# Attention in a two-layer block on one core: a semaphore between half products, two exponentials in one, and block results copied by two engines

## The chip, the cores and the metric

The kernel runs on one core of a Trainium2 chip. The metric is the device time of one execution in microseconds. The kernel before takes 3538.99 us (median of 3 runs, 3538.1 to 3539.18).

## The reference

Four stages follow each other, with the same weights in both rounds: attention, a perceptron with squared relu, attention, the perceptron again.

```python
def _A_ref(x, wqkv, wo):                 # S=2048 rows, D=640, H=32 heads of 20
    qkv = (x @ wqkv).reshape(B, S, 3, H, Dh).transpose(2, 0, 3, 1, 4)
    q, k, v = qkv[0], qkv[1], qkv[2]
    scores = jnp.einsum("bhqd,bhkd->bhqk", q, k) * (Dh ** -0.5)
    p = _softmax(scores, axis=-1)
    o = jnp.einsum("bhqk,bhkd->bhqd", p, v)
    return o.transpose(0, 2, 1, 3).reshape(B, S, D) @ wo
...
x = A_x
x = x + _A_ref(_layernorm(x, axis=-1), A_wqkv, A_wo)
x = x + _B_ref(_layernorm(x, axis=-1), B_w1, B_b1, B_w2, B_b2)   # relu(x w1 + b1)^2 w2 + b2
x = x + _A_ref(_layernorm(x, axis=-1), A_wqkv, A_wo)
x = x + _B_ref(_layernorm(x, axis=-1), B_w1, B_b1, B_w2, B_b2)
```

## The kernel before

All is float32. Products that need the accuracy are made from a high and a low part of each operand.

Only the attention is touched by the change. It runs over 32 blocks in each layer. A block `t` is a group of four heads and 512 queries, and it goes through 16 key tiles of 128 keys. The passage of one key tile is called a step here. A step holds:

- four score products, one for each head of the group (`score`, the product is line 596). The 128 keys of the tile are the stationary operand, the 512 queries the moving one. A head has 62 rows in the contraction: 60 of the high and low parts, and 2 that subtract the row's maximum. Heads 0 and 2 lie on partitions 0 to 63 of the array, heads 1 and 3 on partitions 64 to 127, so two products run beside each other. The results go to PSUM banks 0 to 3, in turn (`ps_st`).
- four exponentials on ScalarE (line 603), one for each of these banks, 128 x 512 each, into the tiles `e`.
- the weighted values of the step before (`pv`, line 608): for each head the 128 x 32 values against the exponentials. The four heads take four groups of 32 columns of the array, and all add up in bank 7 over the 16 steps of a block. One row of each group adds up the exponentials, which the division needs.
- products for the row maxima of later blocks (`by_queries`, line 481), with queries as stationary operand and keys as moving one, in banks 4 to 6. VectorE takes the maximum of each. In a step there are two products over 512 keys, one on either half of the partitions (`smax`, the maximum is line 493), and two half products over 256 keys each, which share one bank (`smax_half`, line 521): the first half product fills the left half of the bank from partitions 0 to 63, the second the right half from partitions 64 to 127.

The order of all these instructions is written out by hand, since TensorE takes its instructions in the order of the program. The table `ORDERS` holds strings. In a string `a` is the next score on partitions 0 to 63 (head 0, then head 2), `b` the next on partitions 64 to 127 (head 1, then head 3), `m` and `n` are the full products for maxima on partitions 0 to 63 and 64 to 127, `u` and `w` the two half products on partitions 0 to 63 and 64 to 127, and `V` is `pv` for the step before. The string in use nearly everywhere is number 12, and eight of its letters and a `V` make up a step:

```python
12: "mbubanawV" * 8,
```

Between `u` and `w` stands an instruction without work on VectorE: the function `smax_half` puts a `nop` there that waits for `u` (line 517 in the profile), and `w` waits for this `nop`. Two products from different halves of the partitions may not write to one bank at the same time, and this keeps them apart.

At the end of a block `finish` copies bank 7 to the tile `o` (line 621, on ScalarE; on VectorE for the last block of a layer), and later steps send out the row of sums, invert it and multiply. The next block's first `V` writes to bank 7 again, so it waits for the copy. `op` in `attention` calls all of this, one letter at a time; `both_heads` (line 1158 and, for its exponential over two banks, line 1165) serves the last block of a layer alone.

Of the kernel before, what the change touches and what calls it, by code (L numbers as in the profile page):

```python
# [10 lines left out]
AF = mybir.ActivationFunctionType  # L11
# [13 lines left out]
QB = 512  # L25
# [7 lines left out]
SCALE = DH ** -0.5  # L33
NBLK = NG * NQB
# [5 lines left out]
def tile_layers(  # L40
# [11 lines left out]
    nc = tc.nc  # L52
# [10 lines left out]
    def name(p):  # L63
        n_alloc[0] += 1
        return f"{p}{n_alloc[0]}"

    def slot(shape, dtype, label):
        return arena.tile(shape, dtype, tag="slot", name=name(label))

    def dma(eng, dst, src):  # L70

        if dst.dtype == F32R:
            dst = dst.bitcast(F32)
        if src.dtype == F32R:
            src = src.bitcast(F32)
        eng.dma_start(dst, src)
# [4 lines left out]
    banks = psum.tile([P, 8, 512], F32, tag="banks", name="banks")  # L81
# [11 lines left out]
        def coming(self, k):  # L93
            return [self.order[(self.n + 1 + i) % len(self.order)] for i in range(k)]

    ps_st = Ring(0, 1, 2, 3)
    ps_pj = Ring(4, 5, 6, 7)
    ps_q = Ring(0, 1, 2, 3)
    ps_all = Ring(0, 1, 2, 3, 4, 5, 6, 7)
# [154 lines left out]
    def split_to(dst_hi, dst_lo, src):  # L254

        nc.scalar.copy(dst_hi, src)
        nc.vector.tensor_sub(dst_lo, src, dst_hi.bitcast(F32))  # L257
# [12 lines left out]
    def pool_hi(dst, src):  # L270
        nc.gpsimd.tensor_copy(dst, src)  # L271
# [31 lines left out]
    def after(later, earlier, reason="one half of the rows adds to the bank that the other half has left"):  # L303
        tc.add_manual_dep(
            later.ins,
            earlier.ins.name,
            mybir.DependencyInfo(mybir.DependencyClass.Sync, mybir.DependencyReason.DATA),
            reason=reason,
        )
# [115 lines left out]
    weights, e_n = [], []  # L425
# [45 lines left out]
    def maxima(t):  # L471
        if t not in mx_t:
            mx_t[t] = small.tile([P, 4, 4, 6], F32, tag="mx", bufs=14, name=name("mx"))
            if t in PARTLY:
                nc.vector.memset(mx_t[t][:, :, :, :4], LEAST)
        return mx_t[t]

    def by_queries(dst, t, p, sub, c, par, keys=slice(0, QB)):

        b = 64 * par  # L480
        return nc.tensor.matmul(  # L481
            dst,
            q_t[t][b : b + 60, p, sub * P : (sub + 1) * P],
            k_t[t // NQB, c][b : b + 60, p, keys],
            start=True,
            stop=True,
        )
# [7 lines left out]
        )  # L495

    halved = {}

    def two_columns(t):

        if t not in halved:
            halved[t] = True
            nc.gpsimd.memset(maxima(t)[:, :, :, 4:], LEAST)

    def column(*x):

        halved[x] = halved.get(x, 3) + 1
        assert halved[x] < 6
        return halved[x]

    def smax_half(bank, t, p, sub, c, half, par, earlier=None):

        w = QB // 2
        dst = bank[:, par * w : (par + 1) * w]
        m = by_queries(dst, t, p, sub, c, par, slice(half * w, (half + 1) * w))
        if earlier is None:
            mark = nc.vector.nop()
            after(mark, m)
            return mark
        after(m, earlier, "matmuls on two halves of the rows write to one bank in turn")  # L520
        nc.vector.tensor_reduce(  # L521
            maxima(t)[:, p : p + 3 : 2, sub, c if not half else column(t, p, sub)],
            bank.rearrange("q (r k) -> q r k", r=2),
            axis=AX.X,
            op=ALU.max,
        )

    def step_one(t, p, sub, x, par):

        dst = ps_q("sm")  # L530
        res = xtile("rl")[:, :QB]
        by_queries(dst, t, p, sub, x, par)
        nc.scalar.activation(res, dst, AF.Relu)  # L533
        return res
# [48 lines left out]
        done.add(t)  # L583

    free = []

    def score(t, kt, h, es):

        p, par = divmod(h, 2)
        if p not in es:  # L590
            es[p] = weights[len(e_n) % len(weights)]
            e_n.append(t)
        dst = banks[:, free.pop(0), :] if free else ps_st("st")
        b = 64 * par
        assert t in done
        nc.tensor.matmul(  # L596
            dst,
            k_t[t // NQB, kt // 4][b : b + 62, p, (kt % 4) * P : (kt % 4 + 1) * P],
            q_t[t][b : b + 62, p, :],
            start=True,  # L600
            stop=True,
        )
        nc.scalar.activation(es[p][:, par, :], dst, AF.Exp, scale=SCALE)  # L603

    def pv(acc, t, kt, es, heads=(3, 2, 1, 0)):
        for h in heads:
            p, par = divmod(h, 2)
            nc.tensor.matmul(  # L608
                acc[32 * h : 32 * h + 32, :],
                v_t[t // NQB, kt // 8][:, kt % 8, 32 * h : 32 * h + 32],  # L610
                es[p][:, par, :],
                start=(kt == 0),
                stop=(kt == NKT - 1),
            )

    def finish(t, acc):


        g, qb = divmod(t, NQB)
        o = slot([P, 2, QB], F32, "o")  # L620
        (nc.vector.tensor_copy if t == NBLK - 1 else nc.scalar.copy)(o[:, 0, :], acc)
        res = []

        def store(q):
            ot = res.pop().rearrange("p l t -> p (l t)")
            for h in range(4):
                r0 = (4 * g + h) * DH
                dma(q, d_o[r0 : r0 + DH, qb], ot[32 * h : 32 * h + DH])

        if t == NBLK - 1:  # L630

            def invert():
                dst = ps_all("rs")
                nc.tensor.matmul(dst, sums_t, o[:, 0, :], start=True, stop=True)
                nc.vector.reciprocal(o[:, 1, :], dst)

            def divide():
                nc.vector.tensor_mul(o[:, 0, :], o[:, 0, :], o[:, 1, :])
                res.append(slot([P, 2, QB], F32R, "ot"))
                split_to(res[0][:, 0, :], res[0][:, 1, :], o[:, 0, :])  # L640

            return [invert, divide, lambda: store(nc.scalar)]

        few = small.tile([P, 16], F32, tag="few", bufs=2, name=name("few"))
        for h in range(4):
            dma(nc.sync, d_s[t, h : h + 1], o[32 * h + DH : 32 * h + DH + 1, 0, :])

        def load():
            dma(nc.sync, few, d_s[t].rearrange("h (q j) -> (h q) j", j=16))

        def invert():
            nc.gpsimd.tensor_tensor(few, few, minus_t, op=ALU.pow)  # L652

        def spread():
            dma(nc.sync, d_r[t].rearrange("h (q j) -> (h q) j", j=16), few)

        def gather():
            for h in range(4):
                dma(nc.sync, o[32 * h : 32 * h + 32, 1, :], d_r[t, h].partition_broadcast(32))

        def divide():
            ot = slot([P, 2, QB], F32R, "ot")
            nc.gpsimd.tensor_mul(o[:, 0, :], o[:, 0, :], o[:, 1, :])
            pool_hi(ot[:, 0, :], o[:, 0, :])
            pool_lo(ot[:, 1, :], o[:, 0, :], ot[:, 0, :].bitcast(F32))
            res.append(ot)

        return [load, invert, spread, gather, divide, lambda: store(nc.sync)]
# [46 lines left out]
    def qkv(first, x_src, rest, scores):  # L715
# [275 lines left out]
        15: "anbmnanbaabmbnammbnaVbmbmmbVmbananVanmbanVnambmbVanbmnaVnmbaanVmbbanmV",  # L991
        14: "mbbbanmbbmambmVanannaVmbnaaanVbmabnmVanbmbmbVnaanmbVmabmbanVbmannaVn",
        13: "baanmbVmbanambbnbmVanbmnaVnaabnmbVanbmaanVnmbbanaVmnbmabVabbmmnaVm",
        12: "mbubanawV" * 8,
    }

    def attention(first, x_src, first_rows):
# [8 lines left out]
        turn = [4, 5, 6]  # L1006
# [23 lines left out]
        rows = {"next": min(t for t in range(NBLK) if t not in done), "at": None}  # L1030
# [113 lines left out]
        def both_heads(p):  # L1144

            i = state["wide"]
            t, kt = divmod(i, NKT)
            if p == 0 and i > state["begun"]:
                state["begun"] = i
                begin(i)  # L1150
            es = es_of.setdefault(i, {})
            es[p] = weights[len(e_n) % len(weights)]
            e_n.append(t)
            state["bank"] = (state["bank"] + 2) % 6
            dst = banks[:, state["bank"] : state["bank"] + 2, :]
            for par in range(2):
                b = 64 * par
                nc.tensor.matmul(  # L1158
                    dst[:, par, :],
                    k_t[t // NQB, kt // 4][b : b + 62, p, (kt % 4) * P : (kt % 4 + 1) * P],  # L1160
                    q_t[t][b : b + 62, p, :],
                    start=True,
                    stop=True,
                )
            nc.scalar.activation(es[p], dst, AF.Exp, scale=SCALE)  # L1165
            if p:
                state["wide"] += 1

# [9 lines left out]
            state["debt"] -= n  # L1178
            return n

        free.extend((5, 6))
        for o in "abab":
            op(o)
        yield
# [12 lines left out]
        for p in (0, 1, 0):  # L1197
            both_heads(p)
# [361 lines left out]
```

## Time and profile before

| what | value |
|---|---|
| time of the kernel before, median of 3 | 3538.99 us |
| the profiled execution's own time | 3538.19 us |
| its span, first to last instruction | 3536.2 us |
| granted TensorE clock over the span | 1.000 |
| TensorE busy | 3521.2 us (100%) |
| TensorE weight loads busy | 2264.2 us (64%) |
| VectorE busy | 2731.2 us (77%) |
| ScalarE busy | 2652.9 us (75%) |

The two attention stages lie at about 310 to 1370 us and 2070 to 3130 us of the span. In rows of the profile, PE is TensorE's products and PEld its weight loads, DVE is VectorE, ACT is ScalarE, SP is SyncE, and DVEq is VectorE's sequencer, which runs waits. A row of a timeline gives the start in us from the beginning of the span, the length in us, the engine, the line, the operation, and what is written from what. `x2` behind a row means two instructions of the same kind that overlap or touch, shown as one bar. A bar of a product is partly modelled: its start is when TensorE took it up, which can be before its weights have arrived. Several waits have their arrow behind the bar: `[0.21 <-ACT o L621]` says that the engine stood idle for 0.21 us and that ScalarE's write of tile `o` in line 621 ended it.

### The profile page before, as it was taken

Reading aid. Unit: us, or ns where it says so; the run is one execution under the profiler, and the core shown is the slowest. Engines: PE = TensorE matmul, PEld = TensorE weight load, DVE = VectorE, ACT = ScalarE, POOL = GpSimd, SP = SyncE. Lnnn points to the kernel's source line nnn. Section 1 sums busy time; section 2 is a strip of 40 time slices with the busy share of each in tenths; the row PEclk is TensorE's granted clock in tenths of the full one; section 3 lists DMA queues with packets and bytes.
Section 4 is the critical chain, followed back from the end, with each engine's and each line's share of the span. In section 5 each row is a group of like instructions: output and inputs, shape, how many; then the busy total and the mean of one; then the engine's idle time right before and its main releaser. Section 6 shows DMA issues by size and latency. Waiting matters only on the chain.

```text
span 3536.2 us, 70757 instructions
## 1 busy us (share of the span) xinstructions
PE 3521.2 (100%) x26542; PEld 2264.2 (64%) x26542; DVE 2731.2 (77%) x5023; ACT 2652.9 (75%) x5208; POOL 809.5 (23%) x927
## 2 busy tenths in 40 slices
PE   9999999999999999999999999999999999999999
PEld 7897444444444446999988964444444444479998
DVE  8878999999999993456567789999999999824443
ACT  3778999999999995122237789999999999932221
POOL 6531444221221111111153201221211211211110
PEclk9999999999999999999999999999999999999999
DMA  9776555323211136734477652232232111376231
GB/s 304 274 233 175 172 156 157 109 70 82 57 48 49 46 110 209 249 106 111 135 269 249 197 150 76 65 82 61 67 82 59 46 48 43 115 226 238 75 82 38
DMA packets 377413, 452.78 MB, mean 128 GB/s; under 512 B 176642, under 2 KB 223746, under 8 KB 377070
## 3 DMA queue, kind: packets, MB, share of 16 engines
q1 hardware_dynamic: 376254, 445.89, 41.6%
q8 instruction: 209, 3.42, 0.4%
q10 hardware_dynamic: 816, 2.36, 0.2%
q14 instruction: 134, 1.10, 0.1%
HBM read 273.83 MB, written 174.30 MB: 127 GB/s over the span
## 4 chain that ended last, share of the span: by engine, by line
PE 95%; DVE 2%; ACT 1%; DMA 1%; issue 1%; POOL 0%; SPq 0%; DVEq 0%; ACTq 0%
PE banks L608 29%; PE banks L481 22%; PE banks L293 13%; PE banks L596 11%; PE banks L1326 10%; PE banks L331 9%; DVE mx L493 1%; ACT e L603 1%; PE banks L1158 0%; DMA q<-d_qk 0%; ACT e L1165 0%; DVE bst L244 0%; DVE xnT L257 0%; DVE x L252 0%; DMA d_qk<-ev 0%
## 5 line engine op out<-in xcount | busy, mean ns | idle before, releaser
L603 ACT ACTIVATE e<-banks 128x512 f32<-128x512 f32 x3968 | 2034.7, 613 | 10.3 <-PE banks L596 2.2
L493 DVE TENSOR_REDUCE mx<-banks 128x1 f32<-128x512 f32 x2094 | 1346.5, 686 | 187.2 <-PE banks L596 126.6
L481 PE MATMUL banks<-k,q 60*128 60x512 f32 x4568 | 1347.7, 374 | 3.0 <-DVE v L377 1.7
L481 PEld LDWEIGHTS banks<-k,q 60*128 60x128 f32 x4568 | 763.8, 184 | 848.5 <-DVE mx L493 824.8
L596 PE MATMUL banks<-q,k 62*128 62x512 f32 x3968 | 1132.1, 432 | 0.4 <-DVE mx L541 0.4
L608 PE MATMUL banks<-e,vg 128*32 128x512 f32 x8192 | 1091.0, 605 | 1.5 <-ACT e L1165 1.5
L596 PEld LDWEIGHTS banks<-q,k 62*128 62x128 f32 x3968 | 654.5, 184 | 99.8 <-ACT e L603 36.6
L521 DVE TENSOR_REDUCE mx<-banks 128x2 f32<-128x512 f32 x982 | 670.5, 683 | 0.0
L541 DVE CUSTOM_DVE_ANT_0 rl<-banks,rl 128x512 f32<-128x512 f32 x510 | 332.8, 689 | 101.1 <-PE banks L481 91.0
L1311 ACT ACTIVATE r<-banks,b_t 128x512 f32<-128x512 f32 x96 | 66.2, 689 | 420.1 <-PE banks L293 396.3
L331 PE MATMUL banks<-xnT,wqk 64*128 64x512 f32 x2400 | 378.8, 394 | 0.3 <-ACT mark_t L333 0.3
L533 ACT ACTIVATE rl<-banks 128x512 f32<-128x512 f32 x510 | 270.8, 597 | 98.2 <-PE banks L481 89.3
L1326 PE MATMUL banks<-w,h 128*128 128x320 f32 x2304 | 340.4, 309 | 0.0
L1326 PEld LDWEIGHTS banks<-w,h 128*128 128x128 f32 x2304 | 339.2, 188 | 1.2
L293 PE MATMUL banks<-xnT,w 128*128 128x512 f32 x1440 | 329.4, 389 | 0.0
L331 PEld LDWEIGHTS banks<-xnT,wqk 64*128 64x128 f32 x2400 | 286.1, 185 | 34.2 <-issue 2.4
L293 PEld LDWEIGHTS banks<-xnT,w 128*128 128x128 f32 x1440 | 269.6, 188 | 55.3
L608 PEld LDWEIGHTS banks<-e,vg 128*32 128x32 f32 x8192 | 161.1, 108 | 165.5 <-issue 78.4
L652 POOL TENSOR_TENSOR few<-few,minus_t 128x16 f32<-128x16 f32 x62 | 179.8, 2900 | 357.9 <-DMA few<-d_s 352.5
L271 POOL CAST mr<-nt 128x32 fp32r<-128x32 f32 x64 | 13.4, 209 | 963.7 <-DVE nt L567 963.7
L331 PE MATMUL banks<-wv,xnT 64*128 64x320 f32 x1920 | 199.4, 307 | 0.9 <-ACT mark_t L333 0.9
L331 PEld LDWEIGHTS banks<-wv,xnT 64*128 64x128 f32 x1920 | 187.3, 185 | 2.5 <-ACT mark_t L333 1.4
(89 smaller groups left out, 2094.2 us busy)
## 6 DMA issues: line engine op xcount, KB each, us to landing
q<-d_qk SPq DMA_DIRECT2D x242, 240.0 KB
d_qk<-ev SPq DMA_DIRECT2D x80, 512.0 KB
k<-d_qk SPq DMA_DIRECT2D x152, 240.0 KB
x<-d_x SPq DMA_DIRECT2D x84, 320.0 KB
d_qk<-ev SPq DMA_DIRECT2D x80, 256.0 KB
d_o<-ot SPq DMA_DIRECT2D x248, 80.0 KB
ot<-d_o SPq DMA_DIRECT2D x38, 512.0 KB
d_v<-v SPq DMA_DIRECT2D x32, 512.0 KB
```

The source lines that it names most:

```text
L293: nc.tensor.matmul(dst, a, b, start=(n == 0), stop=(n == last))
L331: m = nc.tensor.matmul(ch["dst"][:, :width], *pair, start=first, stop=last)
L481: return nc.tensor.matmul(dst, q_t[t][b : b + 60, p, sub * P : (sub + 1) * P], k_t[t // NQB, c][b : b + 60, p, keys], start=True, stop=True,)
L493: nc.vector.tensor_reduce(maxima(t)[:, 2 * par + p, sub, c : c + 1], dst, axis=AX.X, op=ALU.max)
L521: nc.vector.tensor_reduce(maxima(t)[:, p : p + 3 : 2, sub, c if not half else column(t, p, sub)], bank.rearrange("q (r k) -> q r k", r=2), ...
L533: nc.scalar.activation(res, dst, AF.Relu)
L541: nc.vector.tensor_tensor_reduce(out=r, in0=dst, in1=r, scale=1.0, scalar=LEAST, op0=ALU.add, op1=ALU.max, accum_out=maxima(t)[:, 2 * par ...
L596: nc.tensor.matmul(dst, k_t[t // NQB, kt // 4][b : b + 62, p, (kt % 4) * P : (kt % 4 + 1) * P], q_t[t][b : b + 62, p, :], start=True, stop ...
L603: nc.scalar.activation(es[p][:, par, :], dst, AF.Exp, scale=SCALE)
L608: nc.tensor.matmul(acc[32 * h : 32 * h + 32, :], v_t[t // NQB, kt // 8][:, kt % 8, 32 * h : 32 * h + 32], es[p][:, par, :], start=(kt == 0 ...
L652: nc.gpsimd.tensor_tensor(few, few, minus_t, op=ALU.pow)
L1326: nc.tensor.matmul(dst[:, :HALF], hs[f][:, hx, i * P : (i + 1) * P], w_2.piece(at_2(f0 + f, hw, hf)), start=(f == 0 and (hx, hw) == THREE[0]),
```

## The change

Four edits come together. First, the `nop` on VectorE between the half products goes. The first half product raises a semaphore of its own when it ends, and the second waits for that semaphore on TensorE. Second, the scores get fixed banks: head 1 bank 0, head 3 bank 1, head 0 bank 2, head 2 bank 3. Banks 1 and 2 lie side by side, and the exponentials of heads 3 and 0, which are the second and the third in the new order, become one instruction over 128 x 1024. Third, the order of a step becomes `bumbawnaV`. Fourth, at the end of a block VectorE copies the right half of bank 7's columns and ScalarE the left half. In the last block of a layer VectorE still copies all of it. At the start of an attention stage the first four scores use banks 5, 6, 0 and 1 explicitly, as the fixed banks need it.

```diff
-    ps_st = Ring(0, 1, 2, 3)
...
+    first_half = tc.alloc_semaphore("first_half")
+    firsts_done = [0]
...
         m = by_queries(dst, t, p, sub, c, par, slice(half * w, (half + 1) * w))
         if earlier is None:
-            mark = nc.vector.nop()
-            after(mark, m)
-            return mark
-        after(m, earlier, "matmuls on two halves of the rows write to one bank in turn")
-        nc.vector.tensor_reduce(
+            firsts_done[0] += 1
+            m.then_inc(first_half, 1)
+            tc.no_tile_sem_insts.add(m.ins.name)
+            tc.add_to_no_dep_group(f"first half {firsts_done[0]}", m.ins)
+            return m, firsts_done[0]
+        m_1, n = earlier
+        m.wait_op(first_half, n, "sem-ge")
+        tc.declare_no_dep(m.ins, m_1.ins, reason="waits for the semaphore of the first half")
+        tc.declare_fence(m.ins, group=f"first half {n}")
+        r = nc.vector.tensor_reduce(
...
+        tc.declare_no_dep(r.ins, m_1.ins, reason="waits for the second half, which waits for the first")
...
+    SPOT = {(0, 1): 0, (1, 1): 1, (0, 0): 2, (1, 0): 3}
 
     def score(t, kt, h, es):
 
         p, par = divmod(h, 2)
-        if p not in es:
-            es[p] = weights[len(e_n) % len(weights)]
+        pair = "two" if p == par else "one"
+        if pair not in es:
+            es[pair] = weights[len(e_n) % len(weights)]
             e_n.append(t)
-        dst = banks[:, free.pop(0), :] if free else ps_st("st")
+        alone = bool(free) or pair == "one"
+        es[h] = es[pair][:, 1 - par if p == par else p, :]
+        dst = banks[:, free.pop(0) if free else SPOT[p, par], :]
...
-        nc.scalar.activation(es[p][:, par, :], dst, AF.Exp, scale=SCALE)
+        if alone:
+            nc.scalar.activation(es[h], dst, AF.Exp, scale=SCALE)
+        elif 3 - h in es:
+            nc.scalar.activation(es[pair], banks[:, 1:3, :], AF.Exp, scale=SCALE)
...
         o = slot([P, 2, QB], F32, "o")
-        (nc.vector.tensor_copy if t == NBLK - 1 else nc.scalar.copy)(o[:, 0, :], acc)
+        cut = QB // 2 if t < NBLK - 1 else 0
+        nc.vector.tensor_copy(o[:, 0, cut:], acc[:, cut:])
+        if cut:
+            nc.scalar.copy(o[:, 0, :cut], acc[:, :cut])
...
-        12: "mbubanawV" * 8,
+        12: "bumbawnaV" * 8,
...
-        free.extend((5, 6))
+        free.extend((5, 6, 0, 1))
```

`pv` reads `es[h]` in place of `es[p][:, par, :]`, and `both_heads` fills `es` in the same form.

More of the change, by code (lines that the diff above doesn't have):

```diff
@@ L602, in score @@
         )
-        nc.scalar.activation(es[p][:, par, :], dst, AF.Exp, scale=SCALE)
+        if alone:
+            nc.scalar.activation(es[h], dst, AF.Exp, scale=SCALE)
+        elif 3 - h in es:
+            nc.scalar.activation(es[pair], banks[:, 1:3, :], AF.Exp, scale=SCALE)
     def pv(acc, t, kt, es, heads=(3, 2, 1, 0)):
         for h in heads:
-            p, par = divmod(h, 2)
             nc.tensor.matmul(
@@ L610, in pv @@
                 v_t[t // NQB, kt // 8][:, kt % 8, 32 * h : 32 * h + 32],
-                es[p][:, par, :],
+                es[h],
                 start=(kt == 0),
@@ L1151, in both_heads @@
             es = es_of.setdefault(i, {})
-            es[p] = weights[len(e_n) % len(weights)]
+            e = weights[len(e_n) % len(weights)]
             e_n.append(t)
+            es[2 * p], es[2 * p + 1] = e[:, 0, :], e[:, 1, :]
             state["bank"] = (state["bank"] + 2) % 6
@@ L1164, in both_heads @@
                 )
-            nc.scalar.activation(es[p], dst, AF.Exp, scale=SCALE)
+            nc.scalar.activation(e, dst, AF.Exp, scale=SCALE)
             if p:
```

## The prediction

> **What bounds the kernel now.** I read the page's groups first, then the times of repeated lines, then one step instruction by instruction.
>
> ```profile
> PE 3521.2 (100%) x26542; PEld 2264.2 (64%) x26542; DVE 2731.2 (77%) x5023; ACT 2652.9 (75%) x5208; POOL 809.5 (23%) x927
> L603 ACT ACTIVATE e<-banks 128x512 f32<-128x512 f32 x3968 | 2034.7, 613 | 10.3 <-PE banks L596 2.2
> L521 DVE TENSOR_REDUCE mx<-banks 128x2 f32<-128x512 f32 x982 | 670.5, 683 | 0.0
> ```
>
> TensorE seems busy all the time, ScalarE too while it has exponentials (10.3 us idle ahead of 3968). Both bars hide waits, as the step will show. Line 521 runs once for each pair `u`, `w`: 982 steps carry the new order. Two queries by line, one inside a block and one over 29 blocks, give the step and the block:
>
> ```profile
> L521 DVE TENSOR_REDUCE mx<-banks x14: 681/683/686, 1015.7 to 1042.4; 128x2 f32<-128x512 f32 x14
> L621 ACT COPY o<-banks x29: 616/618/620, 345.2 to 1276.5; 128x512 f32<-128x512 f32 x29
> ```
>
> A step is 26.7 / 13 = 2.054 us, a block 931.3 / 28 = 33.26 us, which is 16 steps and 0.39 us more for the block's end. Now one step from the timeline (order `m b u b a n a w V`), with ScalarE's rows from queries of its own:
>
> ```profile
> 1007.45 0.18 PEld L481 LDWEIGHTS banks<-k,q 60*128 60x128 f32 x1 [0.84 <-DVE mx L493]
> 1007.45 0.49 PE L481 MATMUL banks<-k,q 60*128 60x512 f32 x1
> 1007.45 0.49 PE L596 MATMUL banks<-q,k 62*128 62x512 f32 x1
> 1007.56 0.19 PEld L481 LDWEIGHTS banks<-k,q 60*128 60x128 f32 x1
> 1007.56 0.41 PEld L596 LDWEIGHTS banks<-q,k 62*128 62x128 f32 x2
> 1007.78 0.28 PE L481 MATMUL banks<-k,q 60*128 60x256 f32 x1
> 1007.79 0.50 PE L596 MATMUL banks<-q,k 62*128 62x512 f32 x2
> 1007.98 1.29 DVE L493 TENSOR_REDUCE mx<-banks 128x1 f32<-128x512 f32 x2 [0.18 <-PE banks L596]
> 1008.02 0.40 PE L481 MATMUL banks<-k,q 60*128 60x512 f32 x1
> 1008.06 0.18 PEld L596 LDWEIGHTS banks<-q,k 62*128 62x128 f32 x1
> 1008.17 0.18 PEld L481 LDWEIGHTS banks<-k,q 60*128 60x128 f32 x1
> 1008.26 0.30 PE L481 MATMUL banks<-k,q 60*128 60x256 f32 x1
> 1008.49 0.16 PEld L608 LDWEIGHTS banks<-e,vg 128*32 128x32 f32 x8
> 1008.49 1.07 PE L608 MATMUL banks<-e,vg 128*32 128x512 f32 x8
> 1009.48 0.18 PEld L481 LDWEIGHTS banks<-k,q 60*128 60x128 f32 x1 [0.84 <-DVE mx L493]
> ...
> 1007.40 0.62 ACT L603 ACTIVATE e<-banks 128x512 f32<-128x512 f32 x1
> 1008.02 2.07 ACT L603 ACTIVATE e<-banks 128x512 f32<-128x512 f32 x4
> ...
> L517 DVEq EVENT_SEMAPHORE  x1: 21/21/21, 1008.1 to 1008.1; - x1
> ```
>
> All times below count from the step's start, 1007.45. What I take from it:
> - A product of 512 columns holds its half of the partitions 0.23 (line 596's second product at 1007.79, line 481's next on the same half at 1008.02), one of 256 columns half of that. The first product's weights arrive 0.115 after their load starts (0.335 to the next product on that half, less 0.22).
> - Each half has room for one set of weights ahead: the double bar at 1007.56 is two loads of 0.18, so the second starts at 1007.79, just when the product in front of it has started.
> - `V` starts 0.43 after the load for the second `a` (1008.06 to 1008.49), and the next step about 1.00 after `V`.
> - That load waits. ScalarE's last exponential of the step before ends at 1008.02 and frees the bank, and the load follows 0.04 later. So a loop over two steps closes: first exponential at 0.57, all four done 2.07 later at 2.64, 0.04 to the load, 0.43 to `V`, 1.00 to the next start: 4.11 / 2 = 2.055. This is the 2.054. Both engines have slack, and the waits on each other make the step.
> - `w` is late too: `u` starts at 0.33, the `nop` runs at 0.65, and the load of `w` starts at 0.72. It is last in the order, so only 0.115 + 0.11 and the array's emptying follow it.
>
> **The semaphore and the new order.** The order becomes `b u m b a w n a V`. The two halves still carry equal loads: `u m a a` on partitions 0 to 63, `b b w n` on 64 to 127. But `u` is now second, started together with the first `b`, which is twice as long, and `w` has moved from last to sixth, with `n`, `a` and all of `V` behind it in TensorE's queue. So it matters when `u`'s end is reported. By its own length that would be 0.28 after its columns begin at 0.115, and 0.04 for a waiter: 0.44. The trace has a case like it in the projection, where a product of 320 columns (line 331) stands behind one of 512 on the other half. Line 333 is a copy of two numbers that waits for the last product issued. First without a long neighbour, then with one, each from two queries:
>
> ```profile
> 242.58 0.59 PE L331 MATMUL banks<-wv,xnT 64*128 64x320 f32 x5
> 243.27 0.19 ACT L333 COPY mark_t<-mark_t 1x1 f32<-1x1 f32 x1 [0.71 <-PE banks L331]
> ...
> 2028.96 0.40 PE L481 MATMUL banks<-k,q 60*128 60x512 f32 x1
> 2028.96 0.31 PE L331 MATMUL banks<-wv,xnT 64*128 64x320 f32 x1
> 2029.48 0.19 ACT L333 COPY mark_t<-mark_t 1x1 f32<-1x1 f32 x1 [0.59 <-PE banks L481]
> ```
>
> Alone, the copy starts 0.10 after the short product's bar (243.17). Beside the long one it starts 0.21 after the short bar (2029.27) and 0.12 after the long one (2029.36). So the short product is reported only behind the long one that was issued first. For `u` that means behind `b`. A first pair is seen by VectorE at 0.53 and, its second product, by ScalarE at 0.57. For a weight load that waits for the second of the pair I take 0.58, with 0.55 and 0.61 as ends (0.53 and 0.57 with some 0.02 to 0.04 for the second report and the hop).
>
> From there: `w` starts 0.115 later, at 0.695. Only then is the place for weights ahead free for `n`, whose load starts at 0.695, and that of the second `a` queues behind it. `V` follows 0.43 after these loads, at 1.125, and the next step 1.00 later, at 2.125. Against 2.054 this is 0.071 more: 982 x 0.071 = 70 us. The ends give 2.095 (40 us) and 2.155 (99 us). Undisturbed, `w` would start at 0.57, where the second `b` ends, so the load has to be released by 0.46.
>
> The page "TensorE: Matmul & The Clock Gate" of the Trainium skill says, under "What overlaps and what doesn't", that matmuls start and end strictly in program order. The rows above show this for the ends, with the long product on the lower partitions and the short one on the upper; the change has it the other way round, which they don't show. By the page's rule the sum stays as it is, and were the order kept only in the direction of the rows, the first rival's sum would hold.
>
> **The exponentials.** One of 1024 columns in place of two. The last block of each layer has such instructions back to back (below): 24.4 / 27 = 0.90 each, against 0.98 for two of 0.49. ScalarE's step then takes about 0.49 + 0.90 + 0.48 = 1.87 us. The last exponential ends at 0.57 + 0.49 + 0.90 + 0.61 = 2.57 in place of 2.64, which is 0.45 into a next step of 2.125, while the second `a` can't be loaded before 0.695: cover enough, and no gain while `w` is late. VectorE's three reductions take 3 x 0.60 (the double bar of 1.29 less one of 0.69) and have 0.3 left. The `nop` was 21 ns on VectorE, behind a running reduction: nothing. The fixed banks keep one use of each bank per step. The first four scores of a layer use other banks, twice in the run; that is less than one exponential either way.
>
> **The copies.** Rows for now and for the prices:
>
> ```profile
> L1165 ACT ACTIVATE e<-banks x28: 1068/1238/1405, 1345.2 to 1369.6; 128x1024 f32<-128x1024 f32 x28
> 1372.31 0.69 DVE L621 COPY o<-banks 128x512 f32<-128x512 f32 x1 [36.97 <-DMA ot<-d_o]
> L621 ACT COPY o<-banks 128x512 f32<-128x512 f32 x62 | 38.2, 617 | 0.0
> L257 DVE TENSOR_TENSOR xnT<-banks,xnT 128x512 fp32r<-128x512 f32 x20 | 12.9, 680 | 5.9 <-ACT xnT L256 5.9
> ```
>
> Now a copy delays the exponentials behind it and costs 0.39 per block. Halves of 256 columns lie between half and all of 0.69 and 0.62; I take 0.43 and 0.40. Both read bank 7 on all partitions. In line 257 VectorE's read of a bank waits for ScalarE's read of the same bank (it also needs that result), and I take it that the halves here run one after the other, VectorE's first. VectorE gets to it after its reductions: the first starts at 0.66, since `m` now stands behind `u`, and 3 x 0.60 later it is 2.46, or 0.34 into the next step. Its half ends at 0.77, ScalarE's runs from 0.83 to 1.23, and the next block's first `V` starts at 1.27 in place of 1.125: 0.15. ScalarE's exponentials of that step begin at 0.83 + 0.26 = 1.09, and the last ends at 3.07, one step of 2.27 later 0.80: the second `a` is loaded at 0.84 in place of 0.695: 0.15 again. Together 0.30 against 0.39, times 62: 5 us less. If they run beside each other, the new slack takes them whole: 24 us less. The row's copies for the sums leave up to 0.2 us later; the next use of them is four steps on.
>
> The page "PSUM — Partial Sum Buffer" of the Trainium skill, under "PSUM bank collisions raise a hardware error", says that two engines may not be in one bank and quadrant at once, two reads included. No run here shows that; by it the 5 holds and not the 24.
>
> **Sum.** 3538.2 (the profiled execution, 0.8 under the median, 2 us outside its span) + 70 - 5 = 3603 us.
>
> **Rivals.**
> - *`u` reports by its own length* (other side, faster). Then `w` is released at 0.44, in time, and the loop of ScalarE and the second `a` decides: 2.57 + 0.04 + 0.43 + 1.00 = 4.04 / 2 = 2.02, 0.034 less per step: 33 us. With less slack the block's end costs more: VectorE's half ends at 0.87 of the next step, ScalarE's runs from 0.93 to 1.33, `V` starts at 1.37 in place of 1.02 (0.35), and the exponentials, begun at 1.19, release the second `a` at 0.84 in place of 0.60 (0.24): 0.59 against 0.39, 12 us more. 3538 - 33 + 12 = 3517. For it: other half of the array, own semaphore. Against: the copy at 2029.48. It decides from a release before 0.46; at 0.51 the result would be no change.
> - *The copies run beside each other*: 3603 - 19 = 3584. For: different columns. Against: line 257.
> - *The wait isn't the last thing*, as when the wait holds `w`'s product but not its weights: near 2.06, some 3540. Against: every `<-` of lines 481 and 596 in these rows stands at the load.
>
> **How the numbers follow.** Slower by the first reading, with either form of the copies: 0.87. The first rival: 0.10. No change: 0.03. 0.2% of 3538 is 7 us, about what a measurement can tell. The range takes the slow case with its ends: 40 - 5 less half of the copies' 19 gives 3563, 99 - 5 gives 3632.
>
> **What would show it.** In the changed profile: a step of 2.1 us by line 521; ahead of `w`'s weight load an idle time of about 0.2 us that ends at 0.58, with `n` and `a` behind it; `V` near 1.13; ScalarE idle some 0.25 per step; line 517 gone; VectorE's half copy ending before ScalarE's begins. Wrong would be a step under 2.06, or `w` loaded before 0.5.

## The result

The changed kernel takes 3601.9 us (median of 4 runs, 3601.46 to 3602.59) and the kernel before 3538.55 us in the runs beside it (3537.24 to 3539.18). The ratio is 1.018, with a 95% interval from 1.0162 to 1.0197. The change makes the kernel slower by 63 us. The profiled execution has a span of 3600.1 us at a granted clock of 1.0.

**The profile after.** Lines have moved: 521 is now 527, 481 is 480, 493 is 492, 596 is 607, 603 is 615 (one bank) and 617 (two banks joined), 608 is 621, and 621 is 635 (VectorE's half) and 637 (ScalarE's). First the page: busy time and share by engine, then groups with count, busy time, mean and the idle time ahead of them.

```profile
PE 3584.1 (100%) x26544; PEld 2157.0 (60%) x26544; DVE 2743.7 (76%) x5085; ACT 2595.4 (72%) x4218; POOL 810.4 (23%) x927
L615 ACT ACTIVATE e<-banks 128x512 f32<-128x512 f32 x1988 | 1190.6, 604 | 106.1 <-issue 1.5
L617 ACT ACTIVATE e<-banks 128x1024 f32<-128x1024 f32 x990 | 1011.0, 1021 | 1.6 <-PE banks L607 0.8
L527 DVE TENSOR_REDUCE mx<-banks 128x2 f32<-128x512 f32 x984 | 671.6, 683 | 1.9 <-PE banks L480 1.9
```

TensorE's bar still says 100%, as before, at 63 us more. A busy bar of TensorE doesn't tell whether it waits. ScalarE has more idle time: 106.1 us ahead of its single exponentials, where it was 10.3. So ScalarE no longer sets the step. The queries by line give the step (inside one block) and the block (28 of them):

```profile
L527 DVE TENSOR_REDUCE mx<-banks x14: 682/682/684, 1003.0 to 1030.6; 128x2 f32<-128x512 f32 x14
L635 DVE COPY o<-banks x29: 415/415/416, 345.9 to 1306.2; 128x256 f32<-128x256 f32 x29
```

A step is 27.6 / 13 = 2.123 us (it was 2.054), a block 960.3 / 28 = 34.30 (it was 33.26). Of the block 34.30 - 16 x 2.123 = 0.33 is its end. 62 blocks at 1.04 more make 64 us, which is the whole difference. One step of the changed kernel, `b u m b a w n a V`, from its weight loads, with TensorE's bars and the engines that wait:

```profile
1016.60 0.49 PE L607 MATMUL banks<-q,k 62*128 62x512 f32 x1
1016.60 0.62 PE L480 MATMUL banks<-k,q 60*128 60x256 f32 x2
1017.18 0.18 PEld L480 LDWEIGHTS banks<-k,q 60*128 60x128 f32 x1 [0.17 <-PE banks L480]
1017.18 0.18 PEld L607 LDWEIGHTS banks<-q,k 62*128 62x128 f32 x1
1017.25 0.69 DVE L492 TENSOR_REDUCE mx<-banks 128x1 f32<-128x512 f32 x1 [0.24 <-PE banks L480]
1017.29 0.19 PEld L480 LDWEIGHTS banks<-k,q 60*128 60x128 f32 x1
1017.29 0.39 PE L607 MATMUL banks<-q,k 62*128 62x512 f32 x1
1017.41 0.38 PE L480 MATMUL banks<-k,q 60*128 60x512 f32 x1
1017.62 1.02 ACT L617 ACTIVATE e<-banks 128x1024 f32<-128x1024 f32 x1
1017.72 0.16 PEld L621 LDWEIGHTS banks<-e,vg 128*32 128x32 f32 x8 [0.25 <-issue]
1018.52 0.60 ACT L615 ACTIVATE e<-banks 128x512 f32<-128x512 f32 x1
1018.72 0.18 PEld L607 LDWEIGHTS banks<-q,k 62*128 62x128 f32 x1 [0.84 <-ACT e L617]
1018.72 0.38 PE L480 MATMUL banks<-k,q 60*128 60x256 f32 x1
```

The step starts at 1016.60. The load of `w` waits 0.17 for a product of line 480, which is `u`, and starts at 0.58. The load of `n` follows at 0.69, `V` at 1.12, the next step at 2.12. VectorE's row at 1017.25 is the maximum of `m`, which follows `u` on the same half of the partitions. The last line is the next `u` alone: its bar is 0.38. The view of waits from 700 to 1350 us has the same wait all through, 285 times (total us, times, longest); the kernel before has no wait of these loads (line 481 there) for a product in that view:

```profile
PEld banks L480 <- PE banks L480: 49.0, 285, 0.2
PEld banks L621 <- issue: 70.2, 284, 0.3
```

49.0 / 285 = 0.17 each. `V` then follows 0.43 behind the load of `n`, as it followed 0.43 behind that of the second `a` in the prediction's step. Its loads stand idle for 0.25 of this, for no wait that the profile shows (`issue`).

### The profile page after: what moved, and what is told of

It reads as the page before. It is cut to its first block, busy times and chain, and to the rows that moved or that the text cites. A ratio compares the mean times of both kernels' runs of the same rounds, so it can differ in the third digit from the quotient of the medians.

```text
span 3600.1 us, 69939 instructions
## 1 busy us (share of the span) xinstructions
PE 3584.1 (100%) x26544; PEld 2157.0 (60%) x26544; DVE 2743.7 (76%) x5085; ACT 2595.4 (72%) x4218; POOL 810.4 (23%) x927
## 4 chain that ended last, share of the span: by engine, by line
PE 95%; DVE 2%; DMA 1%; issue 1%; ACT 1%; POOL 0%; SPq 0%; DVEq 0%; POOLq 0%; ACTq 0%
PE banks L621 28%; PE banks L607 18%; PE banks L480 17%; PE banks L292 13%; PE banks L1343 9%; PE banks L330 9%; DMA q<-d_qk 1%; DVE mx L492 1%; PE banks L1175 0%; ACT e L1182 0%; DVE bst L243 0%; ACT o L637 0%; DVE xnT L256 0%; DVE x L251 0%; SPq L76 0%
## 5 line engine op out<-in xcount | busy, mean ns | idle before, releaser
L492 DVE TENSOR_REDUCE mx<-banks 128x1 f32<-128x512 f32 x2092 | 1427.3, 686 | 239.6 <-PE banks L480 236.4
L480 PE MATMUL banks<-k,q 60*128 60x256 f32 (+1 forms) x4570 | 1412.9, 388 | 2.0 <-DMA q<-d_qk 0.6
L615 ACT ACTIVATE e<-banks 128x512 f32<-128x512 f32 x1988 | 1190.6, 604 | 106.1 <-issue 1.5
L607 PE MATMUL banks<-q,k 62*128 62x512 f32 x3968 | 1101.6, 424 | 1.2 <-DVE mx L548 0.7
L607 PEld LDWEIGHTS banks<-q,k 62*128 62x128 f32 x3968 | 589.3, 184 | 839.4 <-ACT e L617 769.1
L617 ACT ACTIVATE e<-banks 128x1024 f32<-128x1024 f32 x990 | 1011.0, 1021 | 1.6 <-PE banks L607 0.8
L480 PEld LDWEIGHTS banks<-k,q 60*128 60x128 f32 x4570 | 698.0, 184 | 184.3 <-PE banks L480 158.7
```

What stands on the lines that cost most here:

```text
L480: return nc.tensor.matmul(dst, q_t[t][b : b + 60, p, sub * P : (sub + 1) * P], k_t[t // NQB, c][b : b + 60, p, keys], start=True, stop=True,)
L492: nc.vector.tensor_reduce(maxima(t)[:, 2 * par + p, sub, c : c + 1], dst, axis=AX.X, op=ALU.max)
L607: nc.tensor.matmul(dst, k_t[t // NQB, kt // 4][b : b + 62, p, (kt % 4) * P : (kt % 4 + 1) * P], q_t[t][b : b + 62, p, :], start=True, stop ...
L615: nc.scalar.activation(es[h], dst, AF.Exp, scale=SCALE)
L617: nc.scalar.activation(es[pair], banks[:, 1:3, :], AF.Exp, scale=SCALE)
```

## The experiments

**The theory.** `u` is issued behind the first `b`, which is twice as long, and is reported only behind it. This releases `w`'s load at 0.58 in place of 0.44, and `n` and `V` behind it are late by the same. The rivals are that TensorE's wait for a semaphore of its own is slow by itself, that the new place of `w` costs by the queue alone, that `u` itself runs late beside `b`, and that one of the two other edits is to blame. All ratios below are to the kernel before, with their 95% intervals; the kernel before took 3538.08 us beside the first four kernels and 3537.91 beside the others.

**1. `u` first.**

```diff
-        12: "bumbawnaV" * 8,
+        12: "ubmbawnaV" * 8,
```

> The changed kernel with `u` ahead of the first `b` instead of behind it (order u b m b a w n a V); the semaphore, the joined exponentials and the half copies stay. Theory (a product is reported only behind the longer one that was issued ahead of it): with nothing ahead of it `u` is reported by its own length, the load of `w` is released at about 0.44 of the step in place of 0.585, `w` starts at 0.57 where the second `b` ends, and the loop of ScalarE and the second `a` decides: a step of 2.02 us in place of 2.125, a block of 32.9 us in place of 34.30, 3517 us in all (3505 to 3530). Rival 1 (TensorE's wait on a semaphore of its own is slow by itself, so the 0.585 is `u`'s own end at 0.40 and a hop of 0.19): the load of `w` stays near 0.585, the step near 2.12, 3600 us. Rival 2 (the sixth place of `w`, with `n`, `a` and `V` behind it, costs by the queue alone): the load of `w` is early, but the step stays over 2.08.

Measured: 3517.28 us, ratio 0.9941 (0.9926 to 0.9956). Two letters that start at the same moment are exchanged, and 85 us go. One step of it, from 1014.88:

```profile
1014.72 1.50 DVE L492 TENSOR_REDUCE mx<-banks 128x1 f32<-128x512 f32 x2
1014.88 0.38 PE L480 MATMUL banks<-k,q 60*128 60x256 f32 x1
1014.88 0.49 PE L607 MATMUL banks<-q,k 62*128 62x512 f32 x1
1015.32 0.32 PEld L480 LDWEIGHTS banks<-k,q 60*128 60x128 f32 x2
1015.45 0.28 PE L480 MATMUL banks<-k,q 60*128 60x256 f32 x1
1015.89 0.16 PEld L621 LDWEIGHTS banks<-e,vg 128*32 128x32 f32 x8 [0.25 <-issue]
1016.89 0.18 PEld L480 LDWEIGHTS banks<-k,q 60*128 60x128 f32 x1 [0.84 <-DVE mx L527]
```

`u` and `b` start together, as in the changed kernel, and their bars are 0.38 and 0.49 in both. But the load of `w` (the first of the double bar at 1015.32) is released at 0.44, 0.06 after the end of `u`'s bar. In the changed kernel it comes 0.20 after a bar of 0.38 would end (1016.98 to 1017.18) and 0.09 after the end of `b`'s bar (1017.09). The same wait on the same semaphore costs nothing here: `w` starts at 0.57, `V` at 1.01, the next step at 2.01. So the first rival falls (no slow hop), and the second too (`w` is sixth here as well).

The third rival, that `u` itself runs late, falls by `m`, which comes behind `u` on the same half. VectorE starts on `m` at 0.65 of the step in both kernels: at 1017.25 in the changed kernel, at 1015.53 here (the double bar from 1014.72 ends at 1016.22, and one reduction takes 0.69). So `u` ran in time, and only its report came late. The trace also keeps the moments at which semaphores are raised. In 982 of the 984 pairs of the changed kernel `u`'s semaphore is raised 0.15 to 0.16 after the end of its own bar, and 0.03 after the report of `b`. In kernel 1 it is raised 0.01 after its own bar, in all 984. In either kernel the load of `w` follows 0.04 later in nearly all of them. The block:

```profile
L637 ACT COPY o<-banks x30: 372/372/372, 345.6 to 1299.8; 128x256 f32<-128x256 f32 x30
```

954.2 / 29 = 32.90 us. At a step of 2.01 about 0.7 of it is the block's end, more than the 0.33 of the changed kernel: I take it that the halves of the copy have less slack to hide in; kernel 7 tries this.

**2. The semaphore alone, old order.**

```diff
 # before.py, smax_half
-            mark = nc.vector.nop()
-            after(mark, m)
-            return mark
-        after(m, earlier, "matmuls on two halves of the rows write to one bank in turn")
+            m.then_inc(first_half, 1)
...
+        m.wait_op(first_half, n, "sem-ge")
```

> The kernel before with the semaphore alone: the wait of `w` goes straight to the semaphore of `u` and the copy of nothing on VectorE goes; order m b u b a n a w V, four single exponentials and the whole copy stay. Theory: `w` is last in the order, only its own product follows it, and the loop of ScalarE and the second `a` sets the step: it stays at 2.055 us and the time at 3538 us (3533 to 3543), with the load of `w` at 0.72 or earlier. Rival 1 (TensorE's wait on its own semaphore is slow by itself): the load of `w` later than 0.72, a step over 2.06, over 3545 us.

Measured: 3537.11 us, ratio 0.9998 (0.9988 to 1.0007): no change. Two steps and the start of a third, from the first load of line 481 in each and the last, which is `w`'s; then the block:

```profile
1015.93 0.18 PEld L481 LDWEIGHTS banks<-k,q 60*128 60x128 f32 x1 [0.84 <-DVE mx L493]
1016.61 0.18 PEld L481 LDWEIGHTS banks<-k,q 60*128 60x128 f32 x1
1018.02 0.18 PEld L481 LDWEIGHTS banks<-k,q 60*128 60x128 f32 x1 [0.84 <-DVE mx L493]
1018.70 0.18 PEld L481 LDWEIGHTS banks<-k,q 60*128 60x128 f32 x1
1020.04 0.18 PEld L481 LDWEIGHTS banks<-k,q 60*128 60x128 f32 x1 [0.84 <-DVE mx L493]
...
L629 ACT COPY o<-banks x30: 620/622/623, 345.6 to 1309.1; 128x512 f32<-128x512 f32 x30
```

`w` is loaded at 0.68 in place of 0.72, and nothing comes of it. The steps alternate, 2.09 and 2.02, and two of them take 4.11, the prediction's loop over two steps. The block is 963.5 / 29 = 33.22. Taking VectorE out of the wait was worth nothing, since `w` was last and off the loop.

**3. The joined exponentials alone, old order.**

```diff
 # before.py, score
+        alone = bool(free) or pair == "one"
...
+        if alone:
+            nc.scalar.activation(es[h], dst, AF.Exp, scale=SCALE)
+        elif 3 - h in es:
+            nc.scalar.activation(es[pair], banks[:, 1:3, :], AF.Exp, scale=SCALE)
```

> The kernel before with the joined exponentials alone (one of 1024 columns in place of the second and third, and the fixed banks that this needs); the copy of nothing on VectorE, the order m b u b a n a w V and the whole copy stay. Theory: ScalarE's last exponential ends 0.07 earlier, so its loop falls to (2.57 + 0.04 + 0.43 + 1.00) / 2 = 2.02, while the load of `w` at 0.72 and the 0.32 from it to `V` and 1.00 after that hold 2.04: a step of 2.03 to 2.04, 15 to 25 us less, 3520 us (3510 to 3532). Rival (the joined exponential costs more than it saves, or the fixed banks make a score wait): no gain, 3538 us or more.

Measured: 3518.32 us, ratio 0.9945 (0.9928 to 0.9961).

```profile
L609 ACT ACTIVATE e<-banks x12: 1017/1017/1020, 1010.7 to 1033.1; 128x1024 f32<-128x1024 f32 x12
L626 ACT COPY o<-banks x30: 603/605/607, 345.3 to 1300.6; 128x512 f32<-128x512 f32 x30
```

A step is 22.4 / 11 = 2.036, a block 955.3 / 29 = 32.94. So this edit, with the fixed banks that it needs, is a gain of 20 us where ScalarE's loop sets the step. It was in the changed kernel too, where nothing of it shows.

**4. Four single exponentials in the changed kernel.**

```diff
-        alone = bool(free) or pair == "one"
+        alone = True
```

> The changed kernel with four single exponentials in place of two single and one joined; order b u m b a w n a V, semaphore and half copies stay. Theory: while the load of `w` at 0.585 holds the step, ScalarE has cover: the last exponential ends 0.07 later, at 0.52 of the next step, ahead of the 0.695 at which the second `a` can be loaded. The step stays at 2.125; at the block's end the second `a` comes up to 0.08 later, 0 to 5 us: 3602 us (3599 to 3609). Rival (the joined exponential is what makes the changed kernel slower): a step under 2.10, under 3585 us.

Measured: 3606.31 us, ratio 1.0193 (1.0178 to 1.0208), 4 us above the changed kernel, whose interval overlaps with this one.

```profile
L527 DVE TENSOR_REDUCE mx<-banks x13: 680/682/684, 1004.3 to 1029.7; 128x2 f32<-128x512 f32 x13
```

The step is 25.4 / 12 = 2.12, as with the joined ones. What saves 20 us in the old order is worth some 4 in the new one, because another wait has become the last. The joined exponential is not what makes the changed kernel slower.

**5. The whole copy back on ScalarE, in the changed kernel.**

```diff
-        cut = QB // 2 if t < NBLK - 1 else 0
-        nc.vector.tensor_copy(o[:, 0, cut:], acc[:, cut:])
-        if cut:
-            nc.scalar.copy(o[:, 0, :cut], acc[:, :cut])
+        (nc.vector.tensor_copy if t == NBLK - 1 else nc.scalar.copy)(o[:, 0, :], acc)
```

> The changed kernel with the block's copy back on ScalarE as a whole; order b u m b a w n a V, semaphore and joined exponentials stay. Theory: of the 34.30 us of a block in the changed kernel 0.32 are its end, and they come from the two halves standing one behind the other (VectorE's from 0.33 to 0.74 of the next step, ScalarE's from 0.82 to 1.19, the next `V` at 1.25). A whole copy of 0.62 that begins near 0.10 ends near 0.72, ahead of `V` at 1.125, and ScalarE's 0.25 of idle time per step take up the delay of the exponentials: a block's end of 0.00 to 0.05, 62 x 0.29 = 18 us less than the changed kernel, 3584 us (3578 to 3590). Rival (a whole copy delays ScalarE as it did before, 0.39 per block): 3606 us.

Measured: 3584.41 us, ratio 1.0132 (1.0116 to 1.0147), 17.5 us below the changed kernel. First the end of a block in the changed kernel, from 997.15, then in this one, from 992.30, and its block:

```profile
997.15 0.18 PEld L607 LDWEIGHTS banks<-q,k 62*128 62x128 f32 x1 [0.84 <-ACT e L617]
997.48 0.41 DVE L635 COPY o<-banks 128x256 f32<-128x256 f32 x1
997.97 0.37 ACT L637 COPY o<-banks 128x256 f32<-128x256 f32 x1 [0.41 <-issue]
998.40 0.16 PEld L621 LDWEIGHTS banks<-e,vg 128*32 128x32 f32 x8 [0.37 <-ACT o L637]
999.39 0.18 PEld L607 LDWEIGHTS banks<-q,k 62*128 62x128 f32 x1 [0.84 <-ACT e L615]
1000.30 0.18 PEld L607 LDWEIGHTS banks<-q,k 62*128 62x128 f32 x1
```

```profile
992.30 0.18 PEld L607 LDWEIGHTS banks<-q,k 62*128 62x128 f32 x1 [0.84 <-ACT e L617]
992.59 0.60 ACT L634 COPY o<-banks 128x512 f32<-128x512 f32 x1
993.43 0.16 PEld L621 LDWEIGHTS banks<-e,vg 128*32 128x32 f32 x8 [0.25 <-ACT o L634]
...
L634 ACT COPY o<-banks x29: 603/603/605, 346.5 to 1298.7; 128x512 f32<-128x512 f32 x29
```

In the changed kernel VectorE's half ends at 0.74 and ScalarE's starts only at 0.82, though ScalarE has been idle for 0.41. `V` follows at 1.25, and the second `a` of the next step at 0.91. The whole copy runs from 0.29 to 0.89, and `V` is at 1.13, where the step has it anyway. The block is 952.2 / 28 = 34.01, or 16 steps and 0.04. Here two halves on two engines finish later than one whole on one. The copy began later than expected (0.29 in place of 0.10); the slack covers it all the same.

**6. ScalarE's half first.**

```diff
+        if cut:
+            nc.scalar.copy(o[:, 0, :cut], acc[:, :cut])
         nc.vector.tensor_copy(o[:, 0, cut:], acc[:, cut:])
-        if cut:
-            nc.scalar.copy(o[:, 0, :cut], acc[:, :cut])
```

> The changed kernel with ScalarE's half of the copy issued first and VectorE's behind it. Theory (one half waits for the other, so the order of the two decides): ScalarE's half begins near 0.10 of the next step and ends near 0.47, VectorE's runs from about 0.52 to 0.93, so `V` at 1.125 isn't held; what stays is VectorE's delay of the reductions by some 0.2 to 0.3 against its slack of 0.3 per step. A block's end of 0.10 to 0.22 in place of 0.32: 6 to 14 us less than the changed kernel, 3592 us (3586 to 3598). Rival 1 (the halves don't wait for each other, ScalarE's half was only late by its place in its queue): both halves begin near 0.1 to 0.35 and overlap. Rival 2 (any use of VectorE for the copy costs what the halves cost now): 3602 us.

Measured: 3594.78 us, ratio 1.0159 (1.0144 to 1.0174), 7 us below the changed kernel.

```profile
995.30 0.18 PEld L607 LDWEIGHTS banks<-q,k 62*128 62x128 f32 x1 [0.84 <-ACT e L617]
995.59 0.39 ACT L636 COPY o<-banks 128x256 f32<-128x256 f32 x1
996.01 0.43 DVE L637 COPY o<-banks 128x256 f32<-128x256 f32 x1 [0.29 <-ACT o L636]
996.49 0.16 PEld L621 LDWEIGHTS banks<-e,vg 128*32 128x32 f32 x8 [0.31 <-DVE o L637]
```

Now VectorE waits for ScalarE: idle for 0.29, it starts 0.03 after ScalarE's half has ended. So the second issued waits for the first, whichever it is, and the copies don't run beside each other: in all 62 blocks of the changed kernel and of this one the second half starts at least 0.03 after the first has ended. It waits for a semaphore of the program. Whether the chip would let the halves overlap without that wait is not shown by any run here. The time is in the range, but not by the mechanism I gave: ScalarE's half runs from 0.29 to 0.68, VectorE's ends at 1.14, and `V` is held to 1.19.

**7. `u` first and the whole copy.** The edits of 1 and 5 together.

> The changed kernel with `u` ahead of the first `b` (order u b m b a w n a V) and with the whole copy on ScalarE; semaphore and joined exponentials stay. With `u` first alone the kernel took 3517.3 us, with a block of 32.90 us, of which 16 steps of 2.012 are 32.19 and the end 0.71. Theory: the end is the halves one behind the other, as in the changed kernel, only without slack; a whole copy costs about what it cost before, 0.35 to 0.45: 62 x 0.3 = 18 us less, 3499 us (3492 to 3506), faster than either kernel. Rival (the end of 0.71 is ScalarE's lack of slack whoever copies): 3513 us or more.

Measured: 3499.66 us, ratio 0.989 (0.9875 to 0.9904), the fastest of all.

```profile
L634 ACT COPY o<-banks x31: 590/605/607, 344.7 to 1323.6; 128x512 f32<-128x512 f32 x31
```

978.9 / 30 = 32.63 a block, 0.27 under `u` first alone. So 0.27 of the block's end of about 0.7 goes with the halves, as expected, and the rival falls; the rest stays with a whole copy too.

**8. The half copies alone, old order.**

```diff
 # before.py, finish
-        (nc.vector.tensor_copy if t == NBLK - 1 else nc.scalar.copy)(o[:, 0, :], acc)
+        cut = QB // 2 if t < NBLK - 1 else 0
+        nc.vector.tensor_copy(o[:, 0, cut:], acc[:, cut:])
+        if cut:
+            nc.scalar.copy(o[:, 0, :cut], acc[:, :cut])
```

> The kernel before with the half copies alone; the copy of nothing on VectorE, the order m b u b a n a w V and four single exponentials stay. Theory: the halves stand one behind the other, VectorE's behind its reductions, so the step's slack doesn't cover them: a block's end of 0.50 to 0.65 in place of 0.39, 7 to 16 us more, 3549 us (3543 to 3556). Rival (half the work for ScalarE is a gain by itself): a block's end under 0.30, under 3532 us.

Measured: 3542.89 us, ratio 1.0013 (1.0004 to 1.0023): slower by 5 us, just under the expected 3543 to 3556. The block's end in the kernel before (step from 1009.48, the next from 1011.61), then here (from 1011.13, the next from 1013.29):

```profile
1009.94 0.62 ACT L621 COPY o<-banks 128x512 f32<-128x512 f32 x1
1010.61 0.16 PEld L608 LDWEIGHTS banks<-e,vg 128*32 128x32 f32 x8 [0.21 <-ACT o L621]
1012.58 0.18 PEld L596 LDWEIGHTS banks<-q,k 62*128 62x128 f32 x1 [0.30 <-ACT e L603]
```

```profile
1011.42 0.41 DVE L622 COPY o<-banks 128x256 f32<-128x256 f32 x1
1011.87 0.37 ACT L624 COPY o<-banks 128x256 f32<-128x256 f32 x1 [0.15 <-DVE o L622]
1012.29 0.16 PEld L608 LDWEIGHTS banks<-e,vg 128*32 128x32 f32 x8 [0.24 <-ACT o L624]
1014.26 0.18 PEld L596 LDWEIGHTS banks<-q,k 62*128 62x128 f32 x1 [0.30 <-ACT e L603]
```

The whole copy ends at 1.08, since ScalarE gets to it only at 0.46; the halves end at 1.11. `V` is at 1.13 and at 1.16, and the second `a` of the next step is loaded at 0.97 in both. I had worked out when the halves end, but not that the whole copy ends nearly as late in the old order. There the halves lose 5 us / 62 = 0.08 per block; in the changed kernel, where ScalarE is early, they lose 0.29. Of the 0.08 these rows show the 0.03 at `V`; where the rest lies isn't shown.

## Why the prediction was right

It said 3603 us, with 3563 to 3632 as the range; measured are 3601.9. By its steps:

- **`u` is reported only behind `b`.** Shown, by the changed kernel (release at 0.58, predicted 0.58) against kernel 1 (0.44, predicted for a report by `u`'s own length), with `m` at 0.65 in both. The rule of the Trainium skill that stood beside the row of line 333 ("TensorE: Matmul & The Clock Gate", "What overlaps and what doesn't": matmuls end in program order) agrees with both. The report in program order holds with the long product on the upper partitions too, which the trace of before had not shown.
- **From there to the step.** `n`'s load at 0.69, `V` at 1.12, the step 2.123 for a forecast of 2.125. The one place that failed: the load of the second `a` does not queue behind that of `n`. It starts with `w`'s at 0.58. It stands behind the waiting `w`, but it goes ahead of `n`, which by the prediction's own reading has to wait until `w` has started on the same half. The sum didn't hang on it, because `n` alone puts `V` at 1.12.
- **The exponentials.** One joined is followed by the next 0.90 later (1017.62 to 1018.52), as forecast. No gain while `w` is late: kernel 4 gives some 4 us where kernel 3 gives 20 without the late `w`.
- **The `nop`.** Nothing, by kernel 2.
- **The copies.** One after the other, VectorE's first: shown by kernels 5 and 6. VectorE's half starts at 0.33 and ScalarE's at 0.82 (forecast 0.34 and 0.83), `V` at 1.25 (1.27). The second `a` of the next step is loaded at 0.91, where 0.84 was forecast: 0.22 late in place of 0.15. A slip of 0.02 is in that forecast: its terms 1.09 + 0.49 + 0.90 + 0.61 make 3.09, not 3.07. The block's end is 0.33 for a forecast of 0.30. What the -5 us of the sum hid is that two opposite things stand in it. The late `w` gives ScalarE so much slack that a whole copy would cost nothing (kernel 5), and the halves give 17.5 us of that back.
- **The first rival.** Its sum of 3517 us is what kernel 1 takes, 3517.28. Its parts were less exact: the step is 2.01, not 2.02, and the block's end about 0.7, not 0.59. These two misses cancel, so the match to 0.3 us is luck.
- **The signs.** Those for the step, for `w`'s load, for `V` and for the copies came as listed, the wait ahead of `w`'s load at 0.17 for "about 0.2". ScalarE's idle time did not: 0.25 per step was forecast, and the page shows 106.1 / 984 = 0.11. The 0.25 was counted from the starts of the exponentials, 0.48 apart for single ones. A bar lasts 0.60, so 0.12 of the slack lies under the last bar.

So the change holds a gain of 20 us in one of its edits (kernel 3), a loss of 17.5 us in the copies against a whole one, and a place in the order that costs 85 us against the same order with two letters exchanged. The three don't add up, since each was measured with the others in place. With the last two mended (kernel 7) the change is a gain of 38 us.

## What to carry to other kernels

When one product on TensorE is to release another, count from the end of the longest product issued ahead of it, not from its own: issue the short one first. An edit that takes time off one engine is worth what the next wait leaves of it, so try each edit alone and again with the others before it is judged (the same joined exponential was worth 20 us and 4). Before a copy is split over two engines, look whether the halves may run beside each other at all, and compare the end of the second half with the end of the whole.

## What the runs showed of the hardware that was not expected

- Weight loads and products of the two halves of the partitions are not always taken up in the order of the program. In the step of the changed kernel the second `a` is loaded at 1017.18 and its bar starts at 1017.29; `n`, which stands ahead of it, is loaded at 1017.29 and starts at 1017.41. The same section of the Trainium skill says that matmuls start in program order as well as end; for the starts, as the bars record them, this trace differs, by 0.12 us, while for the ends it agrees. The bar of the second `a` ends at 1017.68 and that of `n` at 1017.79, and the next two reports of products come at 1017.81 and 1017.84, both behind `n`.
- TensorE's wait for its own semaphore is short: in kernel 1 `w`'s load starts 0.06 after the end of the bar of `u`, and 0.04 after the semaphore is raised, as in the changed kernel.
